# Two first products of a Winograd unit tied behind two fifth products, on one core

## The chip, the cores and the metric

The kernel runs on one core of one Trainium2 chip. The metric is the device time of one execution in microseconds (us). Four runs of the kernel before gave 294.93 to 295.95 us, median 295.65 us.

## The reference, cut to what matters

```python
kv  = einsum('bhsd,bhse->bhde', k, v)          # q, k, v: 8 x 8 x 576 x 64
out = einsum('bhsd,bhde->bhse', q, kv)
rms = sqrt(mean(out * out, axis=-1) + 1e-6)
x   = (out / rms * g_norm)                     # -> 4608 tokens x 512
a, b = x @ w_a, x @ w_b                        # 512 -> 1536 each
result = (a * b) @ w_out                       # 1536 -> 512, float32
```

So there is a linear attention with a norm per head, and then a bilinear feed-forward layer. The feed-forward products are nearly all of the work of TensorE.

## The kernel before, in words

**Units of tokens.** The 4608 tokens are cut into nine units of 512. The first is computed with ordinary products (`std_block`). The other eight (`wino_block`, called with bi = 1 to 8) use a Winograd scheme: seven products in place of eight for a 2 x 2 block product. The "second unit" of the change is bi = 1.

**A unit.** A unit has six column groups, j = 0 to 5, and each group takes seven products. A product is one call of `pe`: four matmuls of 128 x 256 (two for w_a and two for w_b), all at line 868. The code names them p1 to p7, and they are planned in the order p1, p2, p6, p5, p7, p4, p3. p1, p6, p7 and p4 accumulate in the same PSUM bank, X. After p1, p6 and p7 ScalarE copies the running sum out (`ev`, line 436, into the tiles u), and only when that copy is done may the next product add to the bank. After p4 ScalarE casts the sum into c (c21, also printed at line 436), and the bank is free. p2 goes to a bank Y and p5 and p3 to a bank Z; VectorE adds these to the copies (`comb`, line 887). When all four results of a group are there, VectorE multiplies the two halves (line 925) into the tile abt.

**What lies beside it.** While the second unit runs, the attention of the next tokens goes on in slices (`slices`): a matmul of 288 columns (L369, called x here), a square on ScalarE (L379), a matmul that sums the squares over the partitions (L383, called s), a reciprocal root on ScalarE (L387), and a multiplication on VectorE (L392) that writes the tokens and frees both banks. `late_batch` begins each batch with 20 matmuls (L653). VectorE also makes the sums of the weights (L775) and of the outputs (L1025) for the Winograd scheme. The first unit's output product (`o_std`, 48 matmuls of 512 columns at L975, planned in pairs) falls at the end of the second unit, and waits for the output weights wo_t, which come by two DMAs issued by GpSimd (L733). The later units' output products are at L1040.

**What sets the order.** Nothing is issued as it is written. Every step is a `Node` with an engine, an assumed duration, a due time `pr`, the nodes it depends on, and the banks or buffers it takes and frees. `Plan.order` (line 104) plays this through and, whenever an engine is free, picks the node that can start first, by due time among those that can start at once. Banks are handed out in the same play, so a bank's number too is a result of it. The engines' instruction streams are then written in the order that comes out. A dependence between two nodes on the same engine makes no wait on the chip; it only forbids an order.

**Batches and transposed tokens.** From batch 5 on the tokens are computed in tiles (`token_tiles`), stored to DRAM and read back by a transposing DMA on SyncE's queue (L608, L623), and then scaled on ScalarE (L629).

The lines that the change touches are the dependences of p1 (line 898 to 901) and the list of p4 nodes:

```python
p1 = pe(0.0, X, w_at(0, fs), lambda: b11, True,
        xdeps(lo, t0, t0 + n) + ([s_done[1]] if bi == 1 and j else []), [X])
```

Of the kernel before, what the change touches and what calls it, by code (L numbers as in the profile page):

```python
# [137 lines left out]
def kernel(  # L138
# [283 lines left out]
    def mm_us(n, cols):  # L422
        return n * (cols / 2400 + 0.0025)
# [4 lines left out]
    def dve_us(n):  # L428
        return (n + 65) / 960

    def fast_us(n):
        return (n / 2 + 72) / 960

    def either(n, args):
        return [
            ("ACT", act_us(n), lambda: nc.scalar.copy(*args())),  # L436
        ]
# [20 lines left out]
    def xdeps(pairs, ta, tb):  # L458
        return [
            normed[b, p, h]  # L460
            for b in range(B)
            for h in range(2)
            if b * S + h * HF < tb and b * S + (h + 1) * HF > ta
            for p in pairs
        ]
# [3 lines left out]
    o_reads, p5s, s_done = [], [], {}  # L469
# [348 lines left out]
    def wino_block(bi, win, wsum):  # L818
        t0, n = BLOCKS[bi - 1]
        w0, w1 = win  # L820
        c0, c1 = t0 % R, (t0 + n) % R
        b11, b21 = (xp[i][:, :, c0 : c0 + n] for i in range(2))
        b12, b22 = (xp[i][:, :, c1 : c1 + n] for i in range(2))
        lo, hi = (0, 1), (2, 3)
        rd = readers.setdefault(bi, [])
        ab = Buf(RAB)
        t2, t3, t4 = Buf(RT), Buf(RT), Buf(RT)
        tk = plan.add("V", 0.0, w0 - 9, lambda: None, (), [ab])

        def tt(b):  # L830
            return b.tile[:, :, 0:n]

        def t_op(i, op, x, y, o, deps, takes=()):
            return plan.add(
                "DVE", fast_us(2 * n), w0 - 6 + i, lambda: op(o(), x(), y()), deps, takes
            )

        add, sub = nc.vector.tensor_add, nc.vector.tensor_sub
        m3 = t_op(0, sub, lambda: b22, lambda: b12, lambda: tt(t3), xdeps(lo + hi, t0 + n, t0 + 2 * n), [t3])
        m1 = t_op(1, sub, lambda: b12, lambda: b11, lambda: b12, [m3] + xdeps(lo, t0, t0 + n))  # L840
        m2 = t_op(2, sub, lambda: b22, lambda: b12, lambda: tt(t2), [m1], [t2])
        m4 = t_op(3, sub, lambda: b21, lambda: tt(t2), lambda: tt(t4), [m2] + xdeps(hi, t0, t0 + n), [t4])
        rd += [m1, m2, m3, m4]
        muls = {}
        for j in range(NJ):
            fs = slice(j * 128, (j + 1) * 128)
            f2 = slice(HM + j * 128, HM + (j + 1) * 128)
            pr = w0 + (w1 - w0) * j / NJ
            bb = Buf(RB)
            tkb = plan.add("V", 0.0, pr - 3, lambda: None, (), [bb])  # L850
            X = Buf(RQ if (bi == nb and j % 3 == 2) or (bi == 1 and j % 3 == 1) else RO if bi == 1 and j == 0 else RX)
            Y, Z = Buf(RY), Buf(RO if bi == 1 and j in (3, 5) else RY)
            if B5 <= bi < B6:
                X, Y, Z = Buf(RX5), Buf(RY5), Buf(RY5)
            u1, u2, u3 = Buf(RU), Buf(RU), Buf(RU)
            wts = [(wa_t, sums["a"]), (wb_t, sums["b"])]

            def full(b):
                return b.tile[:].rearrange("p (w e) -> p w e", w=2)

            def cs(fi, h, bb=bb):
                return bb.tile[:, 2 * fi + h]

            def pe(off, ps, lhs, rhs, start, deps, takes=(), frees=()):
                def prod():
                    for i, (w, sm) in enumerate(wts):
                        for kc in range(2):
                            nc.tensor.matmul(  # L868
                                ps.tile[:, i * n : (i + 1) * n],
                                lhsT=lhs(w, sm)[:, kc, :],  # L870
                                rhs=rhs()[:, kc, :],
                                start=start and i == 0 and kc == 0,
                                stop=kc == 1,
                                skip_group_check=True,
                            )

                return plan.add("PE", mm_us(4, n), pr + off, prod, deps, takes, frees)

            def ev(off, u, ps, dep):
                return plan.add(  # L880
                    either(2 * n, lambda: (u.tile, full(ps))), 0.0, pr + off, None, [dep], [u]
                )

            def comb(off, fi, h, ps, u, deps, frees, cs=cs, full=full):
                return plan.add(
                    "DVE", dve_us(2 * n), pr + off,
                    lambda: nc.vector.tensor_add(cs(fi, h), full(ps), u.tile),  # L887
                    deps + [tkb], (), frees,
                )

            def w_at(kc, fs):
                return lambda w, sm: w[:, kc : kc + 2, fs]

            def s_at(i, fs=fs):
                return lambda w, sm: sm[:, i, :, fs]

            s1, s2, s3, s4 = ([wsum[w, j][i] for w in "ab"] for i in range(4))
            p1 = pe(
                0.0, X, w_at(0, fs), lambda: b11, True,
                xdeps(lo, t0, t0 + n) + ([s_done[1]] if bi == 1 and j else []), [X],  # L900
            )
            e1 = ev(0.0, u1, X, p1)
            p2 = pe(0.1, Y, w_at(2, fs), lambda: b21, True, xdeps(hi, t0, t0 + n) + p5s[-1:], [Y])
            c11 = comb(0.1, 0, 0, Y, u1, [p2, e1], [Y, u1])
            p6 = pe(0.2, X, s_at(0), lambda: tt(t2), False, [e1, m2] + s2, (), [t2])
            e2 = ev(0.2, u2, X, p6)
            p5 = pe(0.3, Z, w_at(0, f2), lambda: b12, True, [m1] + s1, [Z])
            p5s.append(p5)
            p7 = pe(0.4, X, s_at(1), lambda: tt(t3), False, [e2, m3] + s3, (), [t3])
            e3 = ev(0.4, u3, X, p7)  # L910
            c22 = comb(0.4, 1, 1, Z, u3, [p5, e3], [u3])
            p4 = pe(0.5, X, w_at(2, f2), lambda: tt(t4), False, [e3, m4], (), [t4])
            c21 = plan.add(
                either(2 * n, lambda X=X, cs=cs, full=full: (cs(1, 0), full(X))), 0.0,
                pr + 0.5, None, [p4, tkb], (), [X],
            )
            p3 = pe(0.6, Z, s_at(2), lambda: b22, False, [c22] + s4 + xdeps(hi, t0 + n, t0 + 2 * n))
            c12 = comb(0.6, 0, 1, Z, u2, [p3, e2], [Z, u2])
            rd += [p1, p2, p3, p5]
            outs = [c11, c22, c21, c12]  # L920

            def mul(j=j, bb=bb):
                t = ab.tile[:, j : j + NJ + 1 : NJ, 0 : 2 * n].rearrange("p f (h e) -> p f h e", h=2)
                c = bb.tile[:].rearrange("p (f h) w e -> p f h w e", f=2)
                nc.vector.tensor_mul(t, c[:, :, :, 0], c[:, :, :, 1])  # L925

            m = plan.add("DVE", fast_us(4 * n), pr + 0.6, mul, outs + [tk], (), [bb])
            muls[j] = muls[j + NJ] = m
        return ab, muls
# [251 lines left out]
    ab, muls, reads = std_block((st[0], st[1]))  # L1181
# [3 lines left out]
    for bi in range(1, nb + 1):  # L1185
        o_win = (st[bi] + 1.0, st[bi + 1] - 1.0) if bi < nb else (st[bi] + O_A, st[bi + 1] + O_B)
        if bi == 1:
            o_std(ab, muls, (o_win[0] + 4.0, o_win[1] + 4.0))
            osum = out_sums(st[2] - 10)
        else:  # L1190
            o_block(bi - 1, ab, muls, osum, o_win, 2, (RO, RY5, RY5) if B5 <= bi < B6 else (RO, RY, RY), 1)
        for b in needs[bi]:
            if b > 2:
                loads[b] = load_node(b, at_win[b - 1][0], loads[b - 1], turned.get(b - 2))
            turned[b] = late_batch(b, loads[b], at_win[b])
        ab, muls = wino_block(bi, (st[bi], st[bi + 1]), wsum)
# [40 lines left out]
```

## Time and profile before

| what | value |
|---|---|
| median of four runs | 295.65 us |
| the profiled execution | 295.92 us |
| its span, first to last instruction | 294.10 us |
| TensorE busy, with 2622 matmuls | 287.1 us |
| VectorE / ScalarE busy | 243.3 / 191.3 us |
| granted TensorE clock | 1.000 |
| first Winograd product of the second unit | 33.9 us |
| 20 matmuls of the batch after it (L653) | 79.68 us |

A row of a timeline gives the start, the time taken, the engine, the line, the operation with its tiles, and how many equal instructions were merged. In brackets stands the idle time ahead of it and what ended it. A matmul's row includes its way through the array, so it reaches over the start of the next one: how long TensorE rested must be read from the starts. A row of a table by stage gives the stretch, its length, the busy time of TensorE, its weight loads, VectorE, ScalarE and GpSimd with their instruction counts, and last the granted clock, the DMA share and the rate.

### The profile page before, as it was taken

How to read it: one execution, taken by the hardware profiler on the slowest of the kernel's cores; microseconds unless marked ns; L12 is line 12 of the kernel's file. 1: busy time of each engine (PE TensorE's matmuls, PEld its weight loads, DVE VectorE, ACT ScalarE, POOL GpSimd, SP SyncE). 2: the span in 40 equal slices, each digit the busy share in tenths (PEclk: the TensorE clock that was granted, in tenths of full speed). 3: DMA queues.
4: the chain of work that ended last, by engine and by line, in shares of the span. 5: the costliest groups of instructions: out<-in, count | busy, mean ns of one | idle time of the engine just before them, and what ended most of it. 6: DMA issues, size and time to landing. Idle time of an engine off the chain costs nothing.

```text
span 294.1 us, 6720 instructions
## 1 busy us (share of the span) xinstructions
PE 287.1 (98%) x2622; PEld 237.3 (81%) x2624; DVE 243.3 (83%) x447; ACT 191.3 (65%) x395; POOL 77.8 (26%) x96
## 2 busy tenths in 40 slices
PE   7999999999999999999999999999999999999994
PEld 3645558964788888899988999888988888888883
DVE  5454989997777988799989999979989968698963
ACT  3757766884489677867757866686859546665511
POOL 8945830850390660390000920000000000000000
PEclk9999999999999999999999999999999999999999
DMA  8999999699999699399917999440135000300044
GB/s 177 199 199 200 196 157 170 96 170 166 242 126 161 109 196 170 40 126 212 184 27 135 151 165 157 86 164 19 39 81 172 0 2 0 145 0 2 3 144 142
DMA packets 112643, 36.26 MB, mean 123 GB/s; under 512 B 89060, under 2 KB 108516, under 8 KB 112612
## 3 DMA queue, kind: packets, MB, share of 16 engines
q0 software_dynamic: 77552, 18.44, 66.4%
q1 hardware_dynamic: 34448, 16.70, 26.7%
q10 hardware_dynamic: 612, 0.71, 0.8%
q8 instruction: 20, 0.33, 0.5%
q14 instruction: 11, 0.09, 0.1%
HBM read 37.75 MB, written 14.75 MB: 178 GB/s over the span
## 4 chain that ended last, share of the span: by engine, by line
PE 69%; DVE 10%; DMA 10%; POOL 4%; issue 3%; ACT 2%; SPq 1%; DVEq 0%; ACTq 0%; POOLq 0%
PE bk L868 39%; PE bk L1040 21%; DVE c L887 4%; DMA u<-in_v_dram 4%; DMA wa_t<-in_moe_w_a_dram 4%; PE bk L975 2%; PE bk L403 2%; PE bk L653 2%; DVE abt L925 1%; DMA xs<-xt 1%; SPq L623 1%; POOL as L243 1%; DVE xt L601 1%; PE bk L369 1%; PE bk L383 1%
## 5 line engine op out<-in xcount | busy, mean ns | idle before, releaser
L887 DVE TENSOR_TENSOR c<-bk,u 128x512 f16<-128x512 f32 x144 | 96.2, 684 | 21.8 <-PE bk L868 14.3
L436 ACT COPY u<-bk 128x512 f32<-128x512 f32 x144 | 81.4, 591 | 35.1 <-PE bk L868 28.0
L868 PE MATMUL bk<-xp,wa_t 128*128 128x256 f16 x288 | 55.0, 272 | 0.4 <-ACT c L436 0.3
L868 PE MATMUL bk<-xp,wb_t 128*128 128x256 f16 x288 | 55.0, 273 | 0.0
L868 PEld LDWEIGHTS <-wa_t 128*128 128x128 f16 x384 | 37.0, 98 | 6.1 <-issue 1.1
L868 PEld LDWEIGHTS <-wb_t 128*128 128x128 f16 x384 | 37.5, 98 | 4.4
L1040 PEld LDWEIGHTS <-abt 128*128 128x128 f16 x384 | 37.5, 98 | 4.4
L1040 PE MATMUL bk<-wo_t,abt 128*128 128x256 f16 x288 | 37.1, 273 | 0.0
L436 ACT CAST c<-bk 128x512 f16<-128x512 f32 x48 | 28.2, 587 | 13.5 <-PE bk L868 13.0
L868 PE MATMUL bk<-T,sb 128*128 128x256 f16 x192 | 36.7, 273 | 0.0
L868 PE MATMUL bk<-T,sa 128*128 128x256 f16 x192 | 36.6, 272 | 0.0
L925 DVE TENSOR_TENSOR abt<-c 128x1024 f16<-128x1024 f16 x48 | 32.7, 683 | 0.9
L868 PEld LDWEIGHTS <-sa 128*128 128x128 f16 x288 | 27.9, 98 | 3.9 <-issue 0.3
L868 PEld LDWEIGHTS <-sb 128*128 128x128 f16 x288 | 28.2, 98 | 3.3
L1040 PEld LDWEIGHTS <-as 128*128 128x128 f16 x288 | 28.1, 98 | 3.3
L392 DVE SCALAR_TENSOR_TENSOR xp<-bk,g_col,rs 128x288 f16<-128x288 f32 x40 | 20.2, 512 | 9.9 <-ACT rs L387 9.9
L1072 ACT COPY o_sb<-bk 128x512 f32<-128x512 f32 x30 | 17.6, 586 | 16.4 <-PE bk L1040 15.9
L1040 PE MATMUL bk<-so,as 128*128 128x256 f16 x192 | 25.2, 273 | 0.0
L387 ACT ACTIVATE rs<-bk,eps_t 128x288 f32<-128x288 f32 x40 | 20.0, 506 | 6.0 <-PE bk L383 5.8
L696 POOL DMA_DIRECT2D k_t<-in_k_dram x24 | 21.2, 899 | 1.3 <-DMA u<-in_v_dram 1.0
L690 POOL DMA_DIRECT2D scr<-in_q_dram x12 | 19.6, 1637 | 1.5 <-DMA wb_t<-in_moe_w_b_dram 0.6
L1078 DVE TENSOR_TENSOR o_sb<-bk,o_sb 128x512 f32<-128x512 f32 (+1 forms) x26 | 16.6, 644 | 2.7 <-PE bk L1040 2.5
(109 smaller groups left out, 428.0 us busy)
## 6 DMA issues: line engine op xcount, KB each, us to landing
out_dram<-o_sb SPq DMA_DIRECT2D x20, 256.0 KB, 2.4
scr<-in_q_dram POOLq DMA_DIRECT2D x12, 288.0 KB, 7.7
k_t<-in_k_dram POOLq DMA_DIRECT2D x24, 128.0 KB, 8.7
v_t<-in_v_dram POOLq DMA_DIRECT2D x6, 512.0 KB, 11.2
out_dram<-o_sb SPq DMA_DIRECT2D x18, 128.0 KB, 2.4
wa_t<-in_moe_w_a_dram POOLq DMA_DIRECT2D x6, 256.0 KB, 10.8
wb_t<-in_moe_w_b_dram POOLq DMA_DIRECT2D x6, 256.0 KB, 10.9
wo_t<-in_moe_w_out_dram POOLq DMA_DIRECT2D x2, 768.0 KB, 9.4
```

The lines of the kernel that those rows point to most:

```text
L387: nc.scalar.activation(rs, self.s_ps[p, h][:, 0:HF], AF.Abs_reciprocal_sqrt, bias=eps_t)
L392: nc.vector.scalar_tensor_tensor(out=xcols(p, self.b * S + h * HF, HF), in0=self.x_ps[p, h][:, 0:HF], scalar=g_col, in1=self.rs[p, h], op0 ...
L403: nc.tensor.matmul(ps[:, 0:n], lhsT=w[:, kc, fc * 128 : (fc + 1) * 128], rhs=xcols(kc, 0, n), start=(kc == 0), stop=(kc == KC - 1),)
L436: ("ACT", act_us(n), lambda: nc.scalar.copy(*args())),
L690: nc.gpsimd.dma_start(out=scr[:, :, hl, :].rearrange("p s d -> s p d"), in_=qv[hl])
L696: nc.gpsimd.dma_start(out=kt[:, c], in_=ks[:, :, c, :])
L868: nc.tensor.matmul(ps.tile[:, i * n : (i + 1) * n], lhsT=lhs(w, sm)[:, kc, :], rhs=rhs()[:, kc, :], start=start and i == 0 and kc == 0, st ...
L887: lambda: nc.vector.tensor_add(cs(fi, h), full(ps), u.tile),
L925: nc.vector.tensor_mul(t, c[:, :, :, 0], c[:, :, :, 1])
L1040: nc.tensor.matmul(ps.tile[:, sub * EH : (sub + 1) * EH], lhsT=lhs(slice(j, j + 1))[:, 0, sub * 128 : (sub + 1) * 128], rhs=rhs[:, j, :], ...
L1072: lambda: nc.scalar.copy(o(fi, h), bank(X, every)), [dep], takes, frees,
L1078: nc.vector.tensor_add(o(fi, h, subs), bank(ps, subs), other)
```

## The change

In the second unit only, p1 of group j = 4 also depends on p4 of group j = 0, and p1 of group j = 5 on p4 of group j = 1. For that the p4 nodes of the unit are kept in a list.

```diff
-        muls = {}
+        muls, p4s = {}, []
...
             p1 = pe(
                 0.0, X, w_at(0, fs), lambda: b11, True,
-                xdeps(lo, t0, t0 + n) + ([s_done[1]] if bi == 1 and j else []), [X],
+                xdeps(lo, t0, t0 + n) + (([s_done[1]] if j else []) + p4s[j - 4 : j - 3] * (j > 3) if bi == 1 else []), [X],
             )
...
             c12 = comb(0.6, 0, 1, Z, u2, [p3, e2], [Z, u2])
+            p4s.append(p4)
```

No instruction is added or taken away; the planner gets two more dependences.

## The prediction

> **What bounds the kernel now.** I read the page first, then the windows by stage, then the chain, then the timelines of TensorE, ScalarE and VectorE around the second unit. The page:
>
> ```profile
> PE 287.1 (98%) x2622; PEld 237.3 (81%) x2624; DVE 243.3 (83%) x447; ACT 191.3 (65%) x395; POOL 77.8 (26%) x96
> ...
> PEclk9999999999999999999999999999999999999999
> ...
> PE 69%; DVE 10%; DMA 10%; POOL 4%; issue 3%; ACT 2%; SPq 1%; DVEq 0%; ACTq 0%; POOLq 0%
> ```
>
> TensorE is the bound, but 98% overstates it: matmuls overlap, a 128x256 one lasts 272 ns in its group. The pace is in the chain:
>
> ```profile
> 251.48 7.86 PE bk L868 x72
> ```
>
> That is 109.2 ns each, so one product of four matmuls (one call of `pe`) is 0.437 us. By the same reading a 288-wide one costs 0.1225 us, a 512-wide one of L975 0.216 us, and the 20 of L653 1.12 us. TensorE is idle where a start comes later than the one before plus its pace. From 42 us to the end such gaps sum to only some 1.8 us: 0.83 between 48 and 68, 0.66 between 193 and 195.2, 0.27 at 227. **No reordering can gain more than that; anything it loses is a new gap.** The stages agree:
>
> ```profile
> 60.00:68.00 8.00, 7.78 (x53) 4.99 (x52) 7.49 (x15) 6.37 (x15) 3.59 (x5) 1.00 1.83 167
> ...
> 79.68:125.00 45.32, 45.32 (x433) 40.43 (x431) 36.68 (x68) 34.74 (x75) 20.25 (x22) 1.00 1.37 136
> 125.00:192.00 67.00, 67.00 (x655) 60.52 (x654) 62.65 (x109) 47.27 (x94) 16.39 (x19) 1.00 1.17 138
> ```
>
> The end of the second unit is where TensorE rests; the next 112 us have no gap beyond a few ns. The gaps themselves, TensorE's rows first, then ScalarE, then VectorE:
>
> ```profile
> 59.94 0.38 PE L868 MATMUL bk<-T,sa 128*128 128x256 f16 x2
> ...
> 60.87 0.41 PE L369 MATMUL bk<-qT,kvd 128*128 128x288 bf16 x2
> 61.22 0.38 PE L868 MATMUL bk<-T,sa 128*128 128x256 f16 x2
> ...
> 63.41 0.38 PE L868 MATMUL bk<-T,wb_t 128*128 128x256 f16 x2
> 63.89 0.28 PE L369 MATMUL bk<-qT,kvd 128*128 128x288 bf16 x1
> ...
> 66.87 0.29 PE L383 MATMUL bk<-sq,ones 128*128 128x288 bf16 x1
> 67.27 0.28 PE L369 MATMUL bk<-qT,kvd 128*128 128x288 bf16 x1
> ```
>
> ```profile
> 60.58 0.59 ACT L436 COPY u<-bk 128x512 f32<-128x512 f32 x1 [0.29 <-PE bk L868]
> ```
>
> ```profile
> 62.86 0.55 DVE L1025 TENSOR_TENSOR as<-abt 128x768 f16<-128x768 f16 x1
> 63.33 0.51 DVE L392 SCALAR_TENSOR_TENSOR xp<-bk,g_col,rs 128x288 f16<-128x288 f32 x1
> ...
> 65.25 0.94 DVE L775 TENSOR_TENSOR so<-wo_t 128x1536 f16<-128x1536 f16 x1
> 66.11 0.68 DVE L887 TENSOR_TENSOR c<-bk,u 128x512 f16<-128x512 f32 x1
> 66.72 0.50 DVE L392 SCALAR_TENSOR_TENSOR xp<-bk,g_col,rs 128x288 f16<-128x288 f32 x1
> ```
>
> - p7 of the last group (61.22) waits for the eviction of p6: p6 starts at 59.94, ScalarE at 60.58 (+0.64), takes 0.59, and p7 starts 0.05 later. **So 1.28 us is the shortest way from the start of one product in an X bank to the start of the next.** Between lie p3, two attention slices and p6 itself, 1.12 us: 0.16 us of gap (0.055 before p3, 0.104 before p7).
> - The attention slices at 63.89 (gap 0.265) and 67.27 (0.284) need a bank that VectorE's L392 frees: L392 ends at 63.84 and 67.22, the slices start 0.05 later. L392 is late because VectorE, 7.49 of 8.00 us busy, does other work first: output sums of L1025, and the 0.94 us weight sum of L775.
> - Small: 0.014, 0.061, 0.028, 0.016 before 50.40, 50.89, 58.63, 64.46. With the three above: 0.83.
>
> **The change, part by part.** p1 of j = 4 and 5 gets a dependence on p4 of j = 0 and 1. Both are on TensorE, so no wait is added on the chip: it is an order. And it is not "bank left", as p4 is the last product into the bank, not its eviction. For j = 5 the condition held already (p1.5 stood well behind p4.1). For j = 4 p1 moves from ahead of p4.0 and p6.3 to behind them. Price of the move itself: zero, the same eight instructions (four loads, four matmuls). What waits behind it: p1.4's eviction and then p2.4, p6.4, which come 6 us later in both orders; and the gainer, c21.0, whose p4.0 runs one product (0.437 us) earlier.
>
> All else comes from the planner, which replans from there. The orders of the two built programs (no times in them) differ from that point to about 125 us, then TensorE's last 364 plan entries are in the same order. GpSimd's and SyncE's orders are unchanged, so no load or store passes another. At the end of the unit (p, x, s: product, slice, its norm; O: 512-wide pairs of L975; ' = third unit):
>
> ```
> before: p6.5 p3.4 x2 x3 p7.5 s2 O O O s3 p4.5 x4 p1.0' p1.1' s4 x5 O O O O s5 x6 p3.5
> after:  p6.5 p5.5 x2 x3 p7.5 s2 p3.4 p4.5 s3 O O x4 O O s4 O x5 O O s5 O x6 p3.5
> ```
>
> 1. **p7.5 after p6.5**: one product and two slices between, as before: 1.12 against 1.28, gap 0.16. Stays.
> 2. **p4.5 after p7.5**: new. Between them now lie s2 and p3.4 alone: 0.437 + 0.1225 + 0.437 = 1.00, against 1.28: a new gap of 0.28. Bounds: 0 if evictions were quicker (no row shows it), 0.5 if ScalarE first has to finish the squares of x2 and x3 late. I take 0.28, from the row at 60.58: ScalarE's queue ahead of it is the same.
> 3. **x4**: VectorE now does its L392 directly after c12.4, ahead of the mul of j = 4 (0.60 pace) and the L1025 sum (0.47). From p3.4 to x4 there are p3.4, the 0.28, p4.5, s3 and two O pairs, 2.14 us; c12.4 (ScalarE's lag of 0.64, pace 0.60) and L392 with its release (0.55) need 1.79. Bounds: none to all of 0.265 saved; with 0.35 of room I take all.
> 4. **x6**: the L775 sum of 0.86 us now follows the L392 it preceded. Saves 0.284. x7 is then the tightest: its L392 comes behind L775 and leaves under 0.1 us by my count (bounds 0 to 0.2; I take 0).
> 5. **The small gaps** of the middle (0.12): p4.0, p3.1 and p3.2 have their evictions 0.05 to 0.3 us ahead. 0 to 0.12 remain; I take 0.
> 6. **The output weights**: the second half of wo_t is issued at 53.30 and lands 11.4 us on, at 64.7. TensorE comes to its first user at 48.20 (where the orders part) + 27 products 11.79 + 11 slices 1.35 + L653 1.12 + five O pairs 2.16 + gaps 0.44 = 65.06, before 65.14. 0.35 us of room: price 0, at most 0.2.
> 7. **Third unit's p1.0' and p1.1'** move from 64 to after all O pairs, 74.3 (65.06 + 19 pairs 8.20 + five slices 0.61 + p3.5 0.44); two O pairs took their place, work for work. Their evictions were 10 us early; now p6.0' comes p1, p2, p1.1' and six matmuls of L1040 after (1.97 us) against 1.28. Price 0; without that cover 0.84 each.
> 8. **80 to 125 us**: reordered, but its gap was nil in 45 us while VectorE and ScalarE were at 81% and 77%. I take 0; bounds 0 to 0.3.
>
> Sum: 0.83 - (0.16 + 0.28) = 0.39 us gained by 80 us.
>
> **A rule against it.** The Trainium skill, "TensorE: Matmul & The Clock Gate", section "A second HAM failure mode: psum-queue depth-cycling", says that short idles between groups cycling through PSUM banks can let the clock gate fall to half. Half clock for one of the page's windows of 3.4 us would cost 1.7 us (an estimate from that page) per fall. This trace: granted clock 1.00 in 60 to 68 and in 192 to 196, where one gap is 0.49. The new gap of 0.28 is smaller than that. By the rule +1.7 - 0.4, by the row -0.4; I take the row.
>
> **Does the gain reach the end?** The one late place that could swallow it:
>
> ```profile
> 193.43 0.38 PE L868 MATMUL bk<-xp,wb_t 128*128 128x256 f16 x2
> ...
> 194.14 0.38 PE L868 MATMUL bk<-xp,wa_t 128*128 128x256 f16 x2 [0.33 <-ACT c L436]
> ```
>
> TensorE waits there for transposed tokens that went through VectorE (last normalization at 181.02), a store and a transpose. Its start is set by VectorE's order, which follows TensorE, not by a load: I let the lead pass.
>
> The profiled execution took 295.92, span 294.10 and 1.82 around it; that becomes 295.53. The runs' median is 295.65, 0.27 lower: 295.26, rounded to 295.3.
>
> **Rivals.**
> - *A, likeliest, 0.60*: as summed, 295.3; its own range 294.9 to 295.7 (items 5, 6, 8).
> - *B, 0.12: nothing arrives.* The gap at 194.14 grows by the lead, or the new places cost what the old did (also the case that the edit hardly does anything): 295.65. For it: the DMA part of that chain; against: its releaser is VectorE.
> - *C, 0.19: slower.* The cover of item 7 is gone at the seam of second and third unit: p6.0' and p6.1' wait for evictions that used to be 10 us old, as ScalarE first copies out L975's banks. Price 0.84 each: one lost is 295.3 + 0.84 = 296.1, both 297.0. It decides when p6' starts under 1.28 us after its p1', or when ScalarE is more than 0.69 us behind. Against: 1.97 us in the built order.
> - *D, 0.09: faster.* No new gap at p4.5 and the stall at 194 gone too: 0.39 + 0.28 + 0.66 = 1.3, 294.3. Against: nothing in the change touches 194.
>
> **The numbers.** What a measurement can tell here is about 0.3%, 0.89 us. Faster by more: D and a trace of A, 0.10. Slower by more: C less its mild end, 0.16. Within: 0.74. The range 294.5 to 296.5 leaves out most of C (0.13) and about half of D (0.05).
>
> **What would show it.** Right: between 48 and 68 us gaps of about 0.16 at p7.5 and 0.28 at p4.5 and none at x4 and x6; the L653 of the next batch (79.68 before) near 79.5, with one L1040 block more in place of one product done; the gap at 194 unchanged. Wrong: gaps between 74 and 78 (C), a gap ahead of the seventh pair of L975 (item 6), a larger gap at 194 (B), or a clock below 1.00.

## The result, and the profile after

The changed kernel took 295.86 us (median of 43 runs, 295.38 to 296.83), the kernel before 295.34 us in the same comparison (64 runs). The ratio is 1.0016, with a 95% interval of 1.0009 to 1.0023: **slower by about half a microsecond**, where 0.4 us of gain was forecast. It is inside the 0.3% that was set as "no change", but the sign is wrong and clear of the noise.

The two profiled executions happen to be equally long: 295.92 us, span 294.1. Inside them the parts differ. First the stretch that the prediction was about, in the table by stage of the changed kernel (stretch, length, then busy time of TensorE, its weight loads, VectorE, ScalarE, GpSimd, then clock, DMA share, GB/s):

```profile
60.00:68.00 8.00, 7.85 (x51) 4.78 (x50) 8.00 (x15) 5.67 (x13) 3.23 (x5) 1.00 1.85 168
...
79.68:125.00 45.32, 45.32 (x433) 40.45 (x431) 37.46 (x70) 35.06 (x76) 22.36 (x24) 1.00 1.47 142
```

TensorE's timeline of the changed kernel in that stretch, then VectorE's:

```profile
59.37 0.38 PE L868 MATMUL bk<-T,sa 128*128 128x256 f16 x2
...
60.24 0.41 PE L369 MATMUL bk<-qT,kvd 128*128 128x288 bf16 x2
60.69 0.38 PE L868 MATMUL bk<-T,sa 128*128 128x256 f16 x2
...
61.46 0.38 PE L868 MATMUL bk<-xp,sb 128*128 128x256 f16 x2
61.96 0.38 PE L868 MATMUL bk<-T,wa_t 128*128 128x256 f16 x2
...
62.51 1.03 PE L976 MATMUL bk<-wo_t,abt 128*128 128x512 f16 x4
63.38 0.29 PE L369 MATMUL bk<-qT,kvd 128*128 128x288 bf16 x1
...
65.04 1.03 PE L976 MATMUL bk<-wo_t,abt 128*128 128x512 f16 x4
...
66.03 0.59 PE L976 MATMUL bk<-wo_t,abt 128*128 128x512 f16 x2
66.46 0.29 PE L369 MATMUL bk<-qT,kvd 128*128 128x288 bf16 x1
```

```profile
62.62 0.50 DVE L392 SCALAR_TENSOR_TENSOR xp<-bk,g_col,rs 128x288 f16<-128x288 f32 x1
...
65.61 0.51 DVE L392 SCALAR_TENSOR_TENSOR xp<-bk,g_col,rs 128x288 f16<-128x288 f32 x1
66.03 0.94 DVE L775 TENSOR_TENSOR so<-wo_t 128x1536 f16<-128x1536 f16 x1
```

p7 of the last group waits 0.20 us (60.24 plus two slices of 0.1225 is 60.49, its start is 60.69), p4 waits 0.28 (61.46 + 0.218 is 61.68, its start is 61.96), and the slices at 63.38 and 66.46 follow the pairs of L976 ahead of them without a gap (62.51 plus four times 0.216, 66.03 plus two), because VectorE now does L392 earlier and L775 later. All gaps from 48 to 70 us sum to 0.48 us, against 0.83 in the same stretch before. The 20 matmuls of the next batch (L653) start at 79.53, where 79.5 was forecast. The order does what the sum said. So the loss is elsewhere, and the end of the two kernels shows it. VectorE's last addition, in the kernel before:

```profile
290.38 0.42 DVE L1078 TENSOR_TENSOR o_sb<-bk,o_sb 128x256 f32<-128x256 f32 x1 [0.23 <-PE bk L1040]
```

and in the changed kernel:

```profile
289.48 0.42 DVE L1079 TENSOR_TENSOR o_sb<-bk,o_sb 128x256 f32<-128x256 f32 x1 [0.23 <-PE bk L1041]
```

The arithmetic ends 0.90 us earlier, and the span is the same. What stands between is the landing of the last store. SyncE's waits after 289 us (waited for; us in all, times, longest), before:

```profile
SPq L1232 <- DMA out_dram<-o_sb: 1.3, 3, 0.7
```

and after:

```profile
SPq L1233 <- DMA out_dram<-o_sb: 2.5, 3, 1.4
```

The DMA queues of the changed kernel between 290.2 and 293.2 us (packets, MB, share of 16 engines; then the last store, with the time from issue to landing):

```profile
q1 hardware_dynamic: 271, 0.24, 24.5%
q10 hardware_dynamic: 150, 0.13, 13.5%
q14 instruction: 1, 0.01, 1.7%
...
out_dram<-o_sb SPq DMA_DIRECT2D x1, 128.0 KB, 3.0
```

There is one packet of queue 14, **a fetch of code** (the profile calls the queue's kind "instruction"): 8 KB, from 291.43 to 292.26 us. All but two of the last store's packets are through by 291.44; of these two the first, 1 KB, starts at 292.26, as the fetch ends, and the store takes 3.0 us to land. In the kernel before, the same window has no packet of queue 14; its fetch comes at 294.46, when all is over.

The section on the change says that no instruction is added or taken away. That is not so: the planner made another order, and the other order needs one more semaphore instruction (a wait for another engine) on VectorE (579 to 580 in the built program) and one on ScalarE (599 to 600). The page has it as 6722 instructions against 6720. The theory, **F**: VectorE's code is fetched in blocks, and one more instruction brings the last fetch in front of the end, onto the last store. The rival, **O**: the new order itself loses the time, and the fetch is a coincidence of one profile.

### The profile page after: what moved, and what is told of

It reads as the page before. It is cut to its first block, busy times and chain, and to the rows that moved or that the text cites. A ratio compares the mean times of both kernels' runs of the same rounds, so it can differ in the third digit from the quotient of the medians.

```text
span 294.1 us, 6722 instructions
## 1 busy us (share of the span) xinstructions
PE 287.3 (98%) x2622; PEld 237.6 (81%) x2624; DVE 243.3 (83%) x447; ACT 191.1 (65%) x395; POOL 76.9 (26%) x96
## 4 chain that ended last, share of the span: by engine, by line
PE 86%; DMA 7%; POOL 3%; issue 1%; DVE 1%; ACT 0%; ACTq 0%; POOLq 0%
PE bk L868 49%; PE bk L1041 25%; DMA wa_t<-in_moe_w_a_dram 4%; DMA u<-in_v_dram 4%; PE bk L976 4%; PE bk L403 2%; PE bk L653 2%; PE bk L369 1%; POOL as L243 1%; PE bk L568 1%; PE bk L383 1%; POOL so L243 1%; POOL wa_t L309 1%; POOL wb_t L310 1%; POOL abt L243 0%
## 5 line engine op out<-in xcount | busy, mean ns | idle before, releaser
L392 DVE SCALAR_TENSOR_TENSOR xp<-bk,g_col,rs 128x288 f16<-128x288 f32 x40 | 20.2, 511 | 8.7 <-ACT rs L387 8.5
```

The source lines that it names most:

```text
L392: nc.vector.scalar_tensor_tensor(out=xcols(p, self.b * S + h * HF, HF), in0=self.x_ps[p, h][:, 0:HF], scalar=g_col, in1=self.rs[p, h], op0 ...
```

## The experiments

**One more VectorE instruction in the kernel before.**

```diff
-    nc.vector.memset(one, 1.0)
+    [nc.vector.memset(one, 1.0) for _ in range(1+1)]
```

> The kernel before, with one more VectorE instruction: the memset of a 1x1 constant is written twice, among the first memsets. The order of all other work is that of the kernel before. Theory F (code fetch): the changed kernel has one VectorE and one ScalarE instruction more than the kernel before, and that moves VectorE's last fetch of code (8 KB on queue 14) from behind the end into the landing of the last store, where it holds one packet for 0.8 us. Then this kernel is slower than the kernel before by 0.8 to 1.3 us, near 296.3, and its trace shows the fetch at 290 to 293 us. Theory O (order): the changed order itself loses the time, and the fetch is a coincidence of one profile: this kernel stays within 0.2 us of the kernel before, 295.3.

Measured: 296.19 us, ratio 1.0035 (1.0023 to 1.0048) to the kernel before, which has 295.12 in this comparison: +1.07 us for a write of four bytes at the start. All engines' orders, but for the doubled memset, are those of the kernel before. Its queues between 290.2 and 293.2 us, and SyncE's wait:

```profile
q14 instruction: 1, 0.01, 1.3%
...
out_dram<-o_sb SPq DMA_DIRECT2D x1, 128.0 KB, 2.9
```

```profile
SPq L1232 <- DMA out_dram<-o_sb: 2.4, 3, 1.4
```

The fetch is at 291.85, and the last store's tail is as long as in the changed kernel. F holds; O can't explain it. The longer landing, 2.9 us against 1.8 in the kernel before, is 1.1 us. (The single profiles of the kernels with one, three and eight more each have one gap of TensorE of 0.28 to 0.35 us as well, between 70 and 190 us, which the others lack. The last section comes back to it.)

**Twenty more.** The same line with `range(20+1)`.

> The kernel before, with 20 more of the same 1x1 memset on VectorE, ahead of its first wait for data. Theory F: the fetch comes about 20 VectorE instructions earlier, near 280 us, where it meets no store that the end waits for: within 0.3 us of the kernel before (295.0 to 295.6), though it has more added instructions than the kernel with one. Theory O: the same, 295.3; if instructions as such cost, the cost would be more than in the kernel with one.

Measured: 295.14 us, ratio 1.0000 (0.9988 to 1.0012). The fetch came at 282.33, and the last store lands as it used to, with SyncE's wait back:

```profile
out_dram<-o_sb SPq DMA_DIRECT2D x1, 128.0 KB, 1.8
```

```profile
SPq L1232 <- DMA out_dram<-o_sb: 1.3, 3, 0.6
```

Twenty instructions cost nothing where one cost 1.07 us. It is not the instruction but the place of the fetch.

**Twenty more in the changed kernel.** The same line, in the changed kernel.

> The changed kernel, with 20 more of the same 1x1 memset on VectorE. Theory F: the last fetch moves out of the last store, and the gain of the order (0.9 us at the last matmul in the one profile, 0.4 by my sum) comes through: 294.5 to 295.0, faster than both kernels. Theory O: 295.9 as the changed kernel, or a little more.

Measured: 294.58 us, ratio 0.9977 (0.9967 to 0.9987): 0.54 us under the kernel before, where the changed kernel was 0.52 above it. The fetch is at 279.28. This is the version to keep, as long as nobody changes a line of it.

**One more on ScalarE, as a control.**

```diff
-    nc.scalar.activation(warm, eps_t, AF.Abs_reciprocal_sqrt)
+    [nc.scalar.activation(warm, eps_t, AF.Abs_reciprocal_sqrt) for _ in range(2)]
```

> The kernel before, with one more ScalarE instruction (the early activation that loads the table is written twice). Control for the other instruction that the change adds. Theory F: ScalarE's last fetch was at 273 us and stays near there, so within 0.2 us of the kernel before, 295.3. Theory O: the same. If it is slower by over 0.5 us, the extra ScalarE instruction is the cause and F names the wrong engine.

Measured: 295.25 us, ratio 1.0001 (0.9989 to 1.0013), and the last fetch stays behind the end, at 293.63. So one ScalarE instruction more costs nothing that can be told from zero, and the last fetch follows VectorE's count.

**The change without its extra VectorE instruction.** The constant is written by ScalarE.

```diff
-    nc.vector.memset(one, 1.0)
+    nc.scalar.activation(one, eps_t[0:1], AF.Copy, scale=0.0, bias=1.0)
```

> The changed kernel with VectorE's instruction count brought back to that of the kernel before: the 1x1 constant is written by ScalarE in place of VectorE. The order of all other work is the changed one. Theory F: VectorE's last fetch goes back behind the end (293 to 295 us), and the time falls by about 1.1 us from the changed kernel, to 294.6 to 294.9, under the kernel before by the 0.3 to 0.55 us that the order is worth. Theory O: it stays at 295.9.

Measured: 294.80 us, ratio 0.9987 (0.9977 to 0.9997): 0.42 us under the kernel before, where the changed kernel was 0.52 above it. The fetch is at 293.47, behind the end:

```profile
SPq L1233 <- DMA out_dram<-o_sb: 1.3, 3, 0.7
```

This undoes the one side effect and keeps the order; ScalarE has one instruction more for it, which the control found harmless. The forecast, 295.26 against 295.65, was a ratio of 0.9987.

**Three and eight more: where the fetch does harm.** `range(3+1)` and `range(8+1)` in the kernel before.

> The kernel before with three more 1x1 memsets on VectorE. Theory F: the fetch comes two VectorE instructions earlier than with one (291.85 us there), so around 289.5 to 291, ahead of the packets of the last store; then it holds an earlier store or nothing, and the time is between that of the kernel before and that with one more: 295.1 to 295.8. If each added instruction cost time by itself, it would be slower than with one more (over 296.2).

> The kernel before with eight more 1x1 memsets on VectorE. Theory F: the fetch falls near 287 to 289 us, among stores that the end does not wait for longest: 295.1, as the kernel before, at most 0.3 above it. Theory O (the order alone costs): 295.1 as well.

Measured: three more 295.80 us, ratio 1.0010 (1.0001 to 1.0020), fetch at 289.33, a little ahead of what was expected; eight more 295.53 us, ratio 1.0006 (0.9994 to 1.0017), fetch at 288.69. The kernel before has a median of 295.22 in this comparison. With three more, SyncE's final wait is 1.7 us, between 1.3 and 2.4:

```profile
SPq L1232 <- DMA out_dram<-o_sb: 1.7, 3, 1.2
```

The fetch now meets the three stores ahead of the last one, which take 2.5 to 2.7 us to land against 2.1 to 2.2 in the kernel before. The cost fades as the fetch leaves the last store. (The profile with three more is of the fastest of its 22 runs, 295.08 us, so it may show less than the usual one.) The small rest with eight is not told from zero. That each added instruction costs by itself is refuted.

**The kernel before once more.**

> The kernel before once more, for a second profile of the same program. The stall of 0.49 us ahead of the first product of the seventh unit (194.14 in the first profile) was gone in the changed kernel, and also in the three variants of the kernel before. If it belongs to one execution and not to the order, this profile has under 0.1 us there; if the order of the kernel before makes it, it is back with 0.4 to 0.5.

Measured: one run of 295.11 us, span 293.3. TensorE at the first product of the seventh unit:

```profile
193.21 0.38 PE L868 MATMUL bk<-xp,wb_t 128*128 128x256 f16 x2
193.42 0.38 PE L868 MATMUL bk<-xp,wa_t 128*128 128x256 f16 x2
```

No gap: 0.21 us apart, as two matmuls should be. The stall of 0.49 us at 194.14 was that one execution's. In the second unit the gaps are 0.83 us again.

**All ten profiles side by side.** The last column is the time from the end of VectorE's last addition to the end of the span, one profile each.

| kernel | start of VectorE's last fetch | last store, issue to landing | end of the addition to end of the span |
|---|---|---|---|
| before | 294.46 (behind the end) | 1.8 | 3.33 |
| before once more | 293.91 (behind the end) | 1.8 | 3.31 |
| before, one more on ScalarE | 293.63 (behind the end) | 1.8 | 3.30 |
| changed, without the extra instruction | 293.47 (behind the end) | 1.8 | 3.30 |
| before, one more | 291.85 | 2.9 | 4.20 |
| changed | 291.43 | 3.0 | 4.24 |
| before, three more | 289.33 | 2.2 | 3.49 |
| before, eight more | 288.69 | 2.1 | 3.41 |
| before, twenty more | 282.33 | 1.8 | 3.10 |
| changed, twenty more | 279.28 | 1.8 | 3.11 |

The end depends on the place of the fetch and not on the order: the fetch on the last store costs 0.9 us there in either order.

## Why the prediction was wrong, point by point

**The step that failed** is "so no wait is added on the chip: it is an order", and after it "Price of the move itself: zero, the same eight instructions". The first half is true for TensorE, whose instruction count stays at 5258. But "All else comes from the planner" was followed only for the order in which VectorE and ScalarE work, never for how many instructions they need: the other order costs each a semaphore instruction more, a term that was put at nothing. On VectorE that one moves the fetch onto the last store: 0.9 us at the end of the trace, and +1.07 us in time by the kernel with one more (ratio 1.0035). With the order's 0.9987 that makes 1.0022; measured was 1.0016 (1.0009 to 1.0023). No rival had it. C was slower too, but by another way. That the time lies inside the forecast range all the same is luck: the gain came as forecast, and a loss that nobody had forecast stood against it.

- *p7.5 after p6.5*: 0.16 forecast, 0.20 measured: from p6 at 59.37 to p7 at 60.69 the way took 1.32 us, not 1.28.
- *p4.5 after p7.5*: a new gap of 0.28 forecast, 0.28 measured (61.96). (p4, which the title calls the fifth product, is the sixth in the planned order.)
- *x4 and x6*: 0.265 and 0.284 saved, as forecast, for the reason given. x7 at 67.57 follows without a gap.
- *Small gaps of the middle*: none left between 42 and 60 us.
- *Output weights*: TensorE comes to the second half at 65.04 (forecast 65.06), with no gap.
- *Seam of second and third unit, and 80 to 125 us*: gaps of 0.02 us in all from 70 to 190 us. Rival C did not happen.
- *Sum*: 0.39 forecast; the gaps say 0.83 - 0.48 = 0.35. By time the order is worth 0.13% with the count restored, 0.23% with twenty more, intervals that overlap: 0.4 to 0.7 us. The traces speak for the lower end. From TensorE's first Winograd product of the second unit to its last matmul it takes 255.30 to 255.33 us in the three kernels with the new order, and 255.54 to 255.67 in the three profiles of the old order that have neither the stall at 194 nor the gap of 0.28 to 0.35: 0.2 to 0.4 us. With twenty more the end is 0.2 us shorter as well (the table), which is not the order's doing; the kernel before with twenty more (ratio 1.0000, 0.9988 to 1.0012) is too uncertain to show so little.
- *The clock*: 1.00 in every stretch with work in both kernels. The rule on idles between groups stayed without effect here.
- *Does the gain reach the end?* It reached VectorE's last addition. The question was put only for TensorE's chain, and the place I checked, at 194, was a chance stall of the one profile: 0.66 us of gaps there in the first profile, 0.07 to 0.11 in the nine others. (Rival B had VectorE as the releaser there; the row names ScalarE's cast.) It also flattered the comparison of the two profiles: of the 0.90 us by which the arithmetic ends earlier, 0.59 is this stall. That the earlier end and the longer landing were equal, 0.9 us each, was chance.
- *The half for j = 5*: alone it builds the very orders of the kernel before on TensorE, VectorE and ScalarE, and the half for j = 4 alone those of the changed kernel. It does nothing, as said.

## What to carry to other kernels

When a tuned kernel moves by a few tenths of a per cent, follow the change to the last store before you believe or reject it: compare when the arithmetic ends with when the span ends. Count the instructions of every engine in the two built programs, semaphore instructions too, and look where the instruction queue's packets fall in the last few microseconds. An idea is judged fairly only with that equalized: here one stray instruction hid a gain of about 0.4 us under a loss of about 1 us, and twenty harmless ones brought the gain back.

## What the runs showed of the hardware that was not expected

Code comes by DMA, and a fetch can stand in front of a store. On queue 14 it came in 8 KB packets that took from 0.31 to 1.31 us. VectorE's last one began when 573 to 576 of VectorE's recorded instructions had begun, in all six kernels in which it fell ahead of the end, however many memsets stood at the start: so it moved from 291.85 us (one more) over 289.33 (three), 288.69 (eight) to 282.33 (twenty). In the kernel before the 574th is the last thing that VectorE does before it waits for the end, and the 575th starts at 293.31, behind the last store. In the changed kernel the 575th starts at 289.49, ahead of it.

The Trainium skill, "Runtime: NRT & Kernel Launch", section "Instruction fetch mechanics", calls the cost of such a crossing mostly hidden. By that rule it would be near zero, and for twenty more it was (ratio 1.0000); where the last store is the only thing left it was 1.07 us. That the fetch and the store's last data packet share one of the DMA engines is read from their times: the fetch ends and the packet starts at 292.26 in the changed kernel, and both again at 292.45 in the kernel with one more. It was not tried by itself.

The blocks seem to show inside the kernel too. Between 70 and 290 us, nine VectorE instructions of the ten profiles began 0.3 to 0.7 us later behind their predecessor than the same instruction did in the median of the profiles of that order. Six of the nine, all of 0.3 to 0.4 us, are VectorE's recorded instruction 192, 320, 448 or 576, which lie 128 apart. With one, three and eight more such a stop comes 0.7 to 3.7 us ahead of the gap of TensorE; with three more:

```profile
166.10 0.69 DVE L925 TENSOR_TENSOR abt<-c 128x1024 f16<-128x1024 f16 x1 [0.46 <-DVE c L887]
...
168.04 0.38 PE L868 MATMUL bk<-xp,sa 128*128 128x256 f16 x2 [0.19 <-DVE c L887]
```

So an added instruction may also move a stop of 0.3 us to a place where it costs. That VectorE waits for code there is read from the spacing alone; no run tried it.
